# A decay table from Exps alone or from Exps and products, and the queues of the first chunk's loads

## The chip, the cores and the metric

The kernel runs on one core of a Trainium2 chip. The metric is the device time of one execution in microseconds (us). Most executions of one kernel here agree within 0.3%; all runs named below were in the fast state, except one single look whose state is unknown.

## The reference

A retention layer (4 batches, 8 heads, 768 positions, head size 64) feeds a gated feed-forward layer (3072 tokens, 512 wide, 1536 inside):

```python
for t in range(S):
    state = gamma[None, :, None, None] * state + np.einsum('bhd,bhe->bhde', k[:, :, t], v[:, :, t])
    y[:, :, t] = scale * np.einsum('bhd,bhde->bhe', q[:, :, t], state)
...
gate = 1.0 / (1.0 + np.exp(-(x @ w_gate)))
val = x @ w_val
return (gate * val @ w_out).astype(np.float32)
```

The decay `gamma` differs by head. The kernel works in chunks of 128 positions, six per batch. It scales v by a table that rises with the position (`tabv`, the decay's reciprocal) and the result by one that falls (`taby`, the decay itself, one column per position), so that the products between need no decay.

## The kernel before

Each chunk goes through: loads, transposes of k and q on TensorE, a copy of them to SBUF, the on-chip memory, on ScalarE (`qkT`), scores on TensorE, masks on VectorE, the state's product on TensorE and its cast on ScalarE (`zbd`), the intra products, and `y_out` on VectorE, which multiplies by `taby`. The first chunks are run one by one while the weights are loaded, with filler matmuls (`keep_on`) to keep TensorE's clock up. From chunk 3 on, attention is interleaved with the feed-forward layer.

```python
    nc.sync.dma_start(out=kf, in_=src(k, 0))
    nc.scalar.dma_start(out=qf, in_=src(q, 0))
    load_v(0, nc.sync)
    ...
    def make_taby(cols):
        for p in range(NP):
            nc.scalar.activation(taby[:, p, cols], toky[:, cols], AX.Exp, scale=lgp[:, p:p + 1], bias=lsc)
    ...
    def scale_v(g, eng):          # two SBUF inputs
        eng.tensor_tensor(vs[g], vf[g], tabv[...].to_broadcast([C, H, D]), op=ALU.mult)
    ...
    make_taby(slice(0, 256))
    nc.vector.tensor_copy(kn[0], kf)
    nc.scalar.copy(qn[0], qf)
    keep_on(36)
    transposes(0)
    keep_on(8)
    scale_v(0, nc.vector)
    scores(0); state(0); state_out(0); masks(0)
    keep_on(8)
    make_taby(slice(256, 384))
    transposes(1)
    ...                            # chunk 1: make_taby(slice(384, 512)) in front of transposes(2)
    make_taby(slice(512, 768))     # chunk 2
    nc.scalar.preload_act_table(AX.Sigmoid)
```

All other loads go through GpSimd's queue, in the order of use, with weights between the chunks.

Of the kernel before, what the change touches and what calls it, by code (L numbers as in the profile page):

```python
# [9 lines left out]
F32 = mybir.dt.float32  # L10
BF16 = mybir.dt.bfloat16
I32 = mybir.dt.int32
AX = mybir.ActivationFunctionType
ALU = mybir.AluOpType
# [3 lines left out]
def kernel(  # L18
# [10 lines left out]
    nc = tc.nc  # L29
    B, H, S, D = q.shape  # L30
# [4 lines left out]
    NP = H // 2  # L35
    KT = D_MODEL // 128
    NFF = D_FF // 128
    scale = 1.0 / math.sqrt(D)
    lg = [math.log(1.0 - 2.0 ** (-5.0 - h)) for h in range(H)]

    ctx.enter_context(tc.manual_schedule())
    const = ctx.enter_context(tc.tile_pool(name="const", bufs=1))
# [12 lines left out]
    def src(x, g):  # L55
        b, c = divmod(g, NCH)
        return x[b, :, c * C:(c + 1) * C, :].rearrange("h s d -> s h d")

    def load_v(g, eng):
        vf[g] = ld.tile([C, H, D], F32, tag="vf", name="vf", bufs=8)  # L60
        eng.dma_start(out=vf[g], in_=src(v, g))  # L61

    def load_kq(g):
        kn[g] = ld.tile([C, H, D], BF16, tag="kn", name="kn")
        qn[g] = ld.tile([C, H, D], BF16, tag="qn", name="qn")
        nc.gpsimd.dma_start(out=kn[g], in_=src(k, g))  # L66
        nc.gpsimd.dma_start(out=qn[g], in_=src(q, g))  # L67

    def load_chunk(g):
        load_kq(g)  # L70
        load_v(g, nc.gpsimd)
# [5 lines left out]
    def load_gate_val(s):  # L77
        cols = slice(s * 256, (s + 1) * 256)
        for dst, w in ((wg, moe_w_gate), (wv, moe_w_val)):
            nc.gpsimd.dma_start(out=dst[:, :, cols],  # L80
                                in_=w.rearrange("(kk p) n -> p kk n", p=128)[:, :, cols])
# [6 lines left out]
    kf = const.tile([C, H, D], F32, name="kf")  # L88
    qf = const.tile([C, H, D], F32, name="qf")
    nc.sync.dma_start(out=kf, in_=src(k, 0))  # L90
    nc.scalar.dma_start(out=qf, in_=src(q, 0))
    load_v(0, nc.sync)
    tokv = const.tile([128, NCH], I32, name="tokv")
    nc.gpsimd.iota(tokv, pattern=[[C, NCH]], base=0, channel_multiplier=1)
    ident = const.tile([128, 128], BF16, name="ident")
    make_identity(nc, ident)
    toky = const.tile([128, S], I32, name="toky")
    nc.gpsimd.iota(toky, pattern=[[1, S]], base=0, channel_multiplier=0)
    load_chunk(1)
    causal = const.tile([128, 128], F32, name="causal")  # L100
    nc.gpsimd.memset(causal, 1.0)
# [7 lines left out]
    lgp = const.tile([128, NP], F32, name="lgp")  # L109
    lsc = const.tile([128, 1], F32, name="lsc")  # L110
    nc.vector.memset(lsc, math.log(scale))
    for p in range(NP):
        nc.vector.memset(lgp[0:D, p:p + 1], lg[2 * p])
        nc.vector.memset(lgp[D:128, p:p + 1], lg[2 * p + 1])
    zbd = [const.tile([128, NP, C], BF16, name=f"zbd{i}") for i in range(2)]
    for t in zbd:
        nc.vector.memset(t, 0.0)
    taby = const.tile([128, NP, S], F32, name="taby")

    def make_taby(cols):  # L120
        for p in range(NP):
            nc.scalar.activation(taby[:, p, cols], toky[:, cols], AX.Exp, scale=lgp[:, p:p + 1], bias=lsc)  # L122

    causal4 = causal.unsqueeze(1).to_broadcast([128, NP, 128])

# [7 lines left out]
    def transposes(g):  # L133
        tp = pa.tile([128, 2 * NP, C], BF16, tag="tp", name="tp")
        for i, x in enumerate((kn[g], qn[g])):
            for p in range(NP):
                nc.tensor.transpose(tp[:, i * NP + p, :], pair(x, p), ident)  # L137
        qkT[g] = at.tile([128, 2 * NP, C], BF16, tag="qkT", name="qkT", bufs=3)
        nc.scalar.activation(qkT[g], tp, AX.Copy)  # L139
# [15 lines left out]
    def masks(g):  # L155
        stA[g] = at.tile([128, NP, C], BF16, tag="stA", name="stA")
        stB[g] = at.tile([128, NP, C], BF16, tag="stB", name="stB")
        nc.vector.tensor_tensor(stA[g], sc[g][0], causal4, op=ALU.mult)  # L158
        nc.vector.tensor_tensor(stB[g], sc[g][1], causal4, op=ALU.mult)  # L159
# [8 lines left out]
    def state(g):  # L168
        b, c = divmod(g, NCH)
        if c == 0:  # L170
            zps[b] = pa.tile([128, NP, D], F32, tag="z", name="z", padded_shape=[128, NP, C])
        if c < NCH - 1:
            for p in range(NP):
                for i in range(2):
                    nc.tensor.matmul(zps[b][i * D:(i + 1) * D, p, :], kn[g][:, 2 * p + i, :], vs[g][:, 2 * p + i, :],  # L175
                                     start=(c == 0 and p == 0), stop=True, skip_group_check=True)

    def state_out(g):
        b, c = divmod(g, NCH)
        if c < NCH - 1:  # L180
            for i in range(2):
                half = slice(i * D, (i + 1) * D)
                nc.scalar.copy(zbd[g % 2][half, :, half], zps[b][half])  # L183

    def intra(g):
        first = g % NCH == 0
        for p in range(NP):
            for i, st in enumerate((stA[g], stB[g])):
                nc.tensor.matmul(y[g][i * D:(i + 1) * D, p, :], vs[g][:, 2 * p + i, :], st[:, p, :],  # L189
                                 start=(first and p == 0), stop=True, skip_group_check=True)  # L190
# [60 lines left out]
    def keep_on(n):  # L251
        u = pf.tile([128, 512], F32, tag="ff", name="ff")
        for _ in range(n):
            nc.tensor.matmul(u[:, :128], ident, ident, start=True, stop=True)  # L254


    load_gate_val(0)
    load_chunk(3)
    for s in range(1, NFF // 2):
        load_gate_val(s)  # L260
    load_chunk(4)
    for s in range(4):
        load_out(s)
# [2 lines left out]

    kn[0] = ld.tile([C, H, D], BF16, tag="kn", name="kn")
    qn[0] = ld.tile([C, H, D], BF16, tag="qn", name="qn")
    make_taby(slice(0, 256))
    nc.vector.tensor_copy(kn[0], kf)  # L270
    nc.scalar.copy(qn[0], qf)
    keep_on(36)
# [3 lines left out]
    scores(0)  # L276
    state(0)
    state_out(0)
    masks(0)
    keep_on(8)  # L280
    make_taby(slice(256, 384))
    transposes(1)
    scale_v(1, nc.vector)
    inter(0)
# [6 lines left out]
    masks(1)  # L291
    inter(1)
    keep_on(10)
    make_taby(slice(384, 512))
    transposes(2)
    intra(1)
    scale_v(2, nc.vector)
# [5 lines left out]
    masks(2)  # L303
    inter(2)
    keep_on(12)
    make_taby(slice(512, 768))
    nc.scalar.preload_act_table(AX.Sigmoid)  # L307
    intra(2)
    y_out(2)
    scale_v(3, nc.vector)  # L310
# [62 lines left out]
```

## Time and profile before

| what | value | where |
|---|---|---|
| time | 248.32 us (248.23 to 248.34) | three runs, the median first; a fourth, taken with the result, makes it 248.30 |
| span of the profiled run, mean granted clock | 246.4 us, 0.997 | page, list of cores |
| TensorE busy | 95% | page |
| Exps of the table between chunks | 5.37 us | timeline of ScalarE |
| k, q and v of chunk 0 land at | 4.6, 5.3, 6.6 us | issue plus time to landing |
| scores of chunks 0, 1, 2 start at | 7.54, 11.76, 15.98 us | timeline of TensorE |
| first up matmul | 18.98 us | timeline of TensorE |

In a line of a timeline the first number is the start and the second the duration, in us; then come engine, source line, operation, output and inputs. A bracket at the end gives how long the engine had been idle and what ended that. Source lines shift by 8 between the two kernels: the copy qkT is L139 before and L147 after, the scaling of v L143 and L151.

### The profile page before, as it was taken

The page shows a single profiled execution, that of the slowest core. Times are in us where ns is not written, and L with a number is a line of the kernel's source. Part 1 is how long each engine was busy: PE and PEld are TensorE (multiplying, and loading weights), DVE is VectorE, ACT ScalarE, POOL GpSimd, SP SyncE. Part 2 cuts the span into 40 slices and gives each one's busy share as a digit, 9 for nine tenths or more (in the row PEclk, how much of TensorE's full clock was granted, in tenths as well). Part 3 has the DMA queues.
Part 4 walks back from the last instruction along what each step waited for, and adds up shares of the span by engine and source line. Part 5 has one row for each costly group of instructions (what it writes and reads, how often), then busy time and mean ns, then how long its engine had stood idle before and what let it go on. Part 6 is the DMA issues. An engine that isn't in the chain of part 4 may idle for free.

```text
span 246.4 us, 4449 instructions
## 1 busy us (share of the span) xinstructions
PE 234.1 (95%) x1816; PEld 123.3 (50%) x1816; DVE 101.5 (41%) x168; ACT 106.0 (43%) x191; POOL 91.5 (37%) x111
## 2 busy tenths in 40 slices
PE   7689998997999999999999999999999999999993
PEld 7565644554455554445554445544445554444441
DVE  2565444563446631246631256541256532234300
ACT  7788333425444431454443444342444542233221
POOL 8986574987999912961111001111000000000000
PEclk9999999999999999999999999999999999999998
DMA  9999999999999932994012100002100002200022
GB/s 146 181 198 196 192 213 203 176 208 232 229 174 127 188 80 84 145 180 61 3 41 78 54 3 3 0 17 92 64 0 3 0 0 88 85 0 3 0 85 85
DMA packets 64212, 24.13 MB, mean 98 GB/s; under 512 B 51969, under 2 KB 59649, under 8 KB 64193
## 3 DMA queue, kind: packets, MB, share of 16 engines
q0 software_dynamic: 57616, 16.78, 62.2%
q1 hardware_dynamic: 5536, 6.82, 8.2%
q10 hardware_dynamic: 1040, 0.26, 0.5%
q8 instruction: 14, 0.23, 0.4%
q14 instruction: 6, 0.04, 0.1%
HBM read 28.31 MB, written 6.29 MB: 140 GB/s over the span
## 4 chain that ended last, share of the span: by engine, by line
PE 91%; ACT 7%; issue 1%; DVE 0%; POOL 0%; POOLq 0%; ACTq 0%
PE ff L234 50%; PE ff L244 26%; PE tp L137 4%; PE sA L153 3%; ACT qkT L139 2%; PE y L189 2%; ACT taby L122 2%; PE z L175 2%; PE y L165 2%; PE ff L254 2%; ACT zbd L183 1%; ACT L307 1%; ACT ob L247 0%; ACT gs L238 0%; DVE xT L197 0%
## 5 line engine op out<-in xcount | busy, mean ns | idle before, releaser
L239 DVE TENSOR_TENSOR hT<-gs,ff 128x512 bf16<-128x512 f32 (+2 forms) x76 | 50.1, 660 | 85.6 <-PE ff L234 81.9
L234 PE MATMUL ff<-xT,wg 128*128 128x512 bf16 (+2 forms) x304 | 74.7, 368 | 1.2 <-DVE xT L197 1.1
L234 PE MATMUL ff<-xT,wv 128*128 128x512 bf16 (+2 forms) x304 | 74.6, 368 | 0.0
L238 ACT ACTIVATE gs<-ff 128x512 f32<-128x512 f32 (+2 forms) x76 | 43.6, 573 | 55.4 <-PE ff L234 55.4
L244 PE MATMUL ff<-wo,hT 128*128 128x512 bf16 x288 | 65.0, 379 | 0.0
L234 PEld LDWEIGHTS <-wv 128*128 128x128 bf16 x304 | 29.3, 98 | 33.2
L244 PEld LDWEIGHTS <-hT 128*128 128x128 bf16 x288 | 27.3, 98 | 32.1
L234 PEld LDWEIGHTS <-wg 128*128 128x128 bf16 x304 | 27.4, 98 | 28.4 <-issue 1.4
L143 POOL TENSOR_TENSOR vs<-vf,tabv 128x512 bf16<-128x512 f32 x16 | 16.6, 1058 | 65.0 <-PE y L189 60.1
L247 ACT COPY ob<-ff 128x512 f32<-128x512 f32 x24 | 14.1, 586 | 54.9 <-PE ff L244 50.5
L139 ACT ACTIVATE qkT<-tp 128x1024 bf16<-128x1024 bf16 x24 | 24.6, 1024 | 13.4 <-PE tp L137 13.3
L197 DVE TENSOR_TENSOR xT<-y,taby 128x512 bf16<-128x512 f32 x24 | 16.4, 684 | 20.6 <-PE y L189 20.6
L158 DVE TENSOR_TENSOR stA<-sA,causal 128x512 bf16<-128x512 f32 x24 | 16.5, 687 | 19.9 <-PE sB L153 19.9
L61 POOL DMA_DIRECT2D vf<-in_v_dram x23 | 21.0, 913 | 5.0 <-issue 2.0
L66 POOL DMA_DIRECT2D kn<-in_k_dram x23 | 21.0, 913 | 3.3 <-DMA wo<-in_moe_w_out_dram 1.7
L67 POOL DMA_DIRECT2D qn<-in_q_dram x23 | 20.6, 897 | 2.6 <-DMA wo<-in_moe_w_out_dram 1.7
L183 ACT CAST zbd<-z 64x256 bf16<-64x256 f32 x40 | 14.7, 367 | 12.1 <-PE z L175 11.8
L159 DVE TENSOR_TENSOR stB<-sB,causal 128x512 bf16<-128x512 f32 x24 | 16.3, 680 | 0.0
L153 PE MATMUL sA<-qkT 64*128 64x128 bf16 x96 | 9.5, 219 | 5.5 <-ACT qkT L139 5.4
L153 PEld LDWEIGHTS <-qkT 64*128 64x128 bf16 x192 | 5.4, 94 | 10.6 <-ACT qkT L139 6.8
L254 PE MATMUL ff<-ident 128*128 128x128 bf16 x104 | 9.0, 252 | 1.6 <-POOL ident masks.py:199 1.6
L189 PE MATMUL y<-stA,vs 128*64 128x128 bf16 x96 | 9.9, 222 | 0.0
(36 smaller groups left out, 123.1 us busy)
## 6 DMA issues: line engine op xcount, KB each, us to landing
out_dram<-ob SPq DMA_DIRECT2D x24, 256.0 KB, 2.0
vf<-in_v_dram POOLq DMA_DIRECT2D x23, 256.0 KB, 7.2
kn<-in_k_dram POOLq DMA_DIRECT2D x23, 128.0 KB, 7.2
qn<-in_q_dram POOLq DMA_DIRECT2D x23, 128.0 KB, 7.1
wg<-in_moe_w_gate_dram POOLq DMA_DIRECT2D x6, 256.0 KB, 8.7
wv<-in_moe_w_val_dram POOLq DMA_DIRECT2D x6, 256.0 KB, 9.2
wo<-in_moe_w_out_dram POOLq DMA_DIRECT2D x4, 384.0 KB, 10.7
qf<-in_q_dram ACTq DMA_DIRECT2D x1, 256.0 KB, 4.5
```

The source lines that it names most:

```text
L61: eng.dma_start(out=vf[g], in_=src(v, g))
L66: nc.gpsimd.dma_start(out=kn[g], in_=src(k, g))
L67: nc.gpsimd.dma_start(out=qn[g], in_=src(q, g))
L139: nc.scalar.activation(qkT[g], tp, AX.Copy)
L143: eng.tensor_tensor(vs[g], vf[g], tabv[:, g % NCH, :].unsqueeze(2).to_broadcast([C, H, D]), op=ALU.mult)
L153: nc.tensor.matmul(sc[g][i][:, p, :], t[half, p, :], t[half, NP + p, :], start=True, stop=True)
L158: nc.vector.tensor_tensor(stA[g], sc[g][0], causal4, op=ALU.mult)
L183: nc.scalar.copy(zbd[g % 2][half, :, half], zps[b][half])
L234: nc.tensor.matmul(u[:, lo:hi], w[:, kk, n1 * 128:(n1 + 1) * 128], xT[t][:, kk, lo:hi], start=(kk == 0), stop=(kk == KT - 1))
L238: nc.scalar.activation(gs[:, lo:hi], ps[0][:, lo:hi], AX.Sigmoid)
L239: nc.vector.tensor_tensor(hT[t][:, n1, lo:hi], gs[:, lo:hi], ps[1][:, lo:hi], op=ALU.mult)
L244: nc.tensor.matmul(o, hT[t][:, n1, sm * 128:(sm + 1) * 128], wo[:, n1, :], start=(n1 == 0), stop=(n1 == NFF - 1))
```

## The change

It means to take the table's Exps out of ScalarE's path between chunks: exp(a + 256 d) is exp(a) times a constant of the head, so the columns from 256 on become two products on GpSimd. With that, the second table load can go earlier. The other part moves q of chunk 0 to SyncE's queue, behind k, and v to ScalarE's, behind the first table load, so that k and q come first.

```diff
     nc.sync.dma_start(out=kf, in_=src(k, 0))
-    nc.scalar.dma_start(out=qf, in_=src(q, 0))
-    load_v(0, nc.sync)
+    nc.sync.dma_start(out=qf, in_=src(q, 0))
+    nc.scalar.preload_act_table(AX.Exp)
+    load_v(0, nc.scalar)
...
-    toky = const.tile([128, S], I32, name="toky")
+    toky = const.tile([128, 256], I32, name="toky")
...
+    for p in range(NP):
+        nc.scalar.activation(taby[:, p, 0:256], toky, AX.Exp, scale=lgp[:, p:p + 1], bias=lsc)
+
+    def extend_taby(i):
+        nc.gpsimd.tensor_tensor(taby[:, :, i * 256:(i + 1) * 256], taby[:, :, 0:256],
+                                gup[i].unsqueeze(2).to_broadcast([128, NP, 256]), op=ALU.mult)
...
     load_gate_val(0)
+    extend_taby(1)
     load_chunk(3)
     for s in range(1, NFF // 2):
         load_gate_val(s)
+    extend_taby(2)
     load_chunk(4)
...
     state_out(0)
+    nc.scalar.preload_act_table(AX.Sigmoid)
...
-    make_taby(slice(256, 384))
-    make_taby(slice(384, 512))
-    make_taby(slice(512, 768))
-    nc.scalar.preload_act_table(AX.Sigmoid)
```

More of the change, by code (lines that the diff above doesn't have):

```diff
@@ L96 @@
     make_identity(nc, ident)
-    toky = const.tile([128, S], I32, name="toky")
-    nc.gpsimd.iota(toky, pattern=[[1, S]], base=0, channel_multiplier=0)
+    toky = const.tile([128, 256], I32, name="toky")
+    nc.gpsimd.iota(toky, pattern=[[1, 256]], base=0, channel_multiplier=0)
     load_chunk(1)
@@ L114 @@
         nc.vector.memset(lgp[D:128, p:p + 1], lg[2 * p + 1])
+    gup = {i: const.tile([128, NP], F32, name=f"gup{i}") for i in (1, 2)}
+    for i, t in gup.items():
+        for h in range(H):
+            nc.vector.memset(t[h % 2 * D:(h % 2 + 1) * D, h // 2:h // 2 + 1], math.exp(256 * i * lg[h]))
     zbd = [const.tile([128, NP, C], BF16, name=f"zbd{i}") for i in range(2)]
@@ L118 @@
     taby = const.tile([128, NP, S], F32, name="taby")
-    def make_taby(cols):
-        for p in range(NP):
-            nc.scalar.activation(taby[:, p, cols], toky[:, cols], AX.Exp, scale=lgp[:, p:p + 1], bias=lsc)
+    for p in range(NP):
[3 more added lines that the diff above has]
+                                gup[i].unsqueeze(2).to_broadcast([128, NP, 256]), op=ALU.mult)
     causal4 = causal.unsqueeze(1).to_broadcast([128, NP, 128])
@@ L268 @@
     qn[0] = ld.tile([C, H, D], BF16, tag="qn", name="qn")
-    make_taby(slice(0, 256))
     nc.vector.tensor_copy(kn[0], kf)
```

## The prediction

> **What bounds the kernel now.** I read the page first, then the chain of waits in order of time for the first 25 us, then the timelines of ScalarE, TensorE, VectorE and GpSimd there, and at last the DMA issues one by one. The page says that TensorE is the bound of the whole, and that ScalarE is on the path only for a few per cent:
>
> ```profile
> ## 4 chain that ended last, share of the span: by engine, by line
> PE 91%; ACT 7%; issue 1%; DVE 0%; POOL 0%; POOLq 0%; ACTq 0%
> PE ff L234 50%; PE ff L244 26%; PE tp L137 4%; PE sA L153 3%; ACT qkT L139 2%; PE y L189 2%; ACT taby L122 2%; PE z L175 2%; PE y L165 2%; PE ff L254 2%; ACT zbd L183 1%; ACT L307 1%; ACT ob L247 0%; ACT gs L238 0%; DVE xT L197 0%
> ```
>
> The table's Exps (L122) and the second table load (L307) are together 3% of 246.4 us, some 6 to 7 us. The timeline of ScalarE shows where they stand: between the cast of the state (zbd) and the copy of the next chunk's transposes (qkT), which the scores wait for.
>
> ```profile
> 8.22 0.76 ACT L183 CAST zbd<-z 64x256 bf16<-64x256 f32 x2 [0.74 <-PE z L175]
> 9.01 1.65 ACT L122 ACTIVATE taby<-toky,lsc,lgp 128x128 f32<-128x128 int32 x4
> 10.68 1.02 ACT L139 ACTIVATE qkT<-tp 128x1024 bf16<-128x1024 bf16 x1
> ...
> 13.22 1.65 ACT L122 ACTIVATE taby<-toky,lsc,lgp 128x128 f32<-128x128 int32 x4
> 14.90 1.02 ACT L139 ACTIVATE qkT<-tp 128x1024 bf16<-128x1024 bf16 x1
> ...
> 17.47 2.07 ACT L122 ACTIVATE taby<-toky,lsc,lgp 128x256 f32<-128x256 int32 x4
> 19.57 1.28 ACT L307 ACT_TABLE_LOAD   x1
> 20.86 0.49 ACT L238 ACTIVATE gs<-ff 128x384 f32<-128x384 f32 x1
> ```
>
> What the reader is to see: after zbd there is never a gap, the table follows, then qkT. Columns are start, duration, engine, line. A second resource is full there: page line "DMA" has nines from the start up to about 90 us. Where data come just in time, I find by setting each landing (issue start plus time to landing) beside its first use. The tightest later one is chunk 5's q: its issue on GpSimd, and its use on TensorE:
>
> ```profile
> 32.88 0.87 POOL L67 DMA_DIRECT2D qn<-in_q_dram  x1
> ```
>
> ```profile
> qn<-in_q_dram POOLq DMA_DIRECT2D x1, 128.0 KB, 10.8
> ```
>
> ```profile
> 44.49 0.39 PE L137 MATMUL tp<-ident,kn 128*128 128x128 bf16 x4
> 44.72 0.39 PE L137 MATMUL tp<-ident,qn 128*128 128x128 bf16 x4
> ```
>
> It lands at 32.88 + 10.8 = 43.7 and is used at 44.72, only 1.0 us later. For chunk 5's k it is 31.95 + 10.7 = 42.65 against 44.49, 1.8 us; for chunk 6's q 36.35 + 10.3 = 46.65 against 48.88, 2.2 us; for the weight slices in between 5 us and more.
>
> **What the Trainium skill says.** "ScalarE: Activation LUTs", section "What ACT_TABLE_LOAD costs", gives 1283 ns for a load and about 1380 ns of drain with it. The trace has 1.28 us, and the next ACTIVATE 0.01 us later; no drain shows here, so I count 1.28. "GPSIMD Engine Reference", section 3.1, gives 4497 ns for a two-input fp32 tensor_tensor of 2048 columns, so an estimate of 2.2 us for 1024; the trace's own row (vs on POOL, 512 columns, 1058 ns) gives 2.1, which agrees. "SBUF — State Buffer", section "Who interferes with whom", says that a VectorE instruction with two SBUF inputs and a GpSimd one that reads SBUF exclude each other for a whole instruction. The trace before has no such pair overlapping, so no row shows it. "DMA: Bandwidth & Descriptors", section "Queues, rings and completion order", says that an engine takes turns between rings, which is what putting k and q on one ring and v on another plays with.
>
> **The change part by part.**
> *Removed from ScalarE:* 1.65 + 1.65 + 2.07 = 5.37 us of Exps between chunks, and the table load at 19.57. The first four Exps (2.06 us) stay, and one table load of 1.28 is put in the place of the first removed group.
> *First chunk:* kn is cast at 4.68 when k lands, q's cast starts at 5.35 when the first Exps end, and q lands at 0.80 + 4.5 = 5.3. With the load issued first, ScalarE may be up to 0.45 us earlier, but TensorE's 36 filler matmuls end at 5.6 in any case. v of chunk 0 may land later, and it can hold the first state up. I count 0 ± 0.4.
> *Chunk 1:* after zbd ends at 8.98 comes the load of 1.28 where Exps of 1.65 stood, so qkT(1) starts at 10.3 in place of 10.68: 0.4 gained.
> *Chunk 2:* nothing stands between now. Shifted by 0.4, the transposes end at 13.34, qkT(2) runs 13.35 to 14.4. TensorE still has the intra products and 12 fillers to do, which end at about 14.45. Scores at 14.45 in place of 15.98: 1.5 gained. So the removed 1.65 is hardly worth more than 1.1, because TensorE's own fillers become the bound.
> *End of chunk 2:* the Exps of 2.07 and the load of 1.28 stood beside VectorE's masks and y_out, not alone: the up matmuls waited for xT until 18.98. Only from 19.79 to 20.86 did a sigmoid wait for the load. Working the order of instructions forward with the durations of before (up(0,0) at 17.45, qkT(3) 19.4 to 20.4, scores(3) at 20.5 behind up(0,1), in place of 22.32) gives 1.8; VectorE's v scaling waits for chunk 3's v (11.59 + 7.0 = 18.6) and takes a little back: 1.7 by 24.6.
> *Added to GpSimd:* two products of 2.1 us. The first stands in front of chunk 3's loads, which go out at about 11.5 in place of 9.85. Then wv's first slice (9.12 + 6.6 = 15.7) is still under way, so the DMA engines don't run dry, and later issues wait for landings anyway (0.2 to 1.0 us each from 15.97 on), so the delay is absorbed. The second lies among those waits too. The shorter iota saves some 0.5 us at the first issue, of which 0 to 0.4 reaches the landings. VectorE gets 16 memsets at 0.1 us a step, before k lands: nothing.
> *At 42 to 44 us:* with TensorE 1.7 early, chunk 5's q would be wanted at 43.0 and lands at 43.7 less 0 to 0.4. It stalls 0.3 to 0.7 and leaves 1.0 to 1.4. From there on TensorE is full to the end as before, and nothing more is won.
> *Sum:* 0.4 + 1.1 + 0.2 − 0.5 = 1.2 us; rounded for the first chunk's doubt, 248.3 − 1.1 = 247.2.
>
> **The rivals.**
> *(a) The whole 5.4 + 1.3 us comes off.* The chain of waits books them so. Against it: the fillers and VectorE lie just under it, and the landings cap it at 1.0 to 1.4 whatever the first 25 us give. It would make 242 to 243.
> *(b) The port lock.* The first product runs from about 9.4 to 11.5, and vs(1) on VectorE, with two SBUF inputs, is ready at about 9.6 when chunk 1's v lands. If the product gets in first, vs(1) goes to 11.5, and y_out(0) and masks(1) behind it: masks end at about 14.05 in place of 13.1, scores(2) at 15.25, a gain there of 0.7, about 1.0 by 25 us. Then the stall at chunk 5 is nil, so the end is nearly the same: 247.3 to 247.6. It depends on tenths which is first; I give it six in ten.
> *(c) v of chunk 0 comes late* behind the table load, or q shares its turn with v and lands after 6: the first chunk loses up to 0.8, but much of it lies under (b). 247.5 to 248.3.
> *(d) GpSimd becomes the bound,* its late issues reaching the landings: chunk 5's q later by up to 2 us would make 248 to 250. The waits for landings speak against it.
>
> **Range and chances.** (b) and the sum above give 247.0 to 247.6; (c) stretches it up, more luck with the landings down. Range 246.4 to 248.0. A gain of 2% needs 5 us, which only (a) gives; a loss of 2% needs something that no view shows.
>
> **What would show it.** Right: no L122 behind a zbd in ScalarE's timeline; a table load of 1.28 behind the first zbd; scores(2) at 14.4 to 15.3; up(0,0) near 17.5 to 18.3; chunk 5's q landing within 0.5 us of 43.7 and TensorE waiting there, or just not; from 50 us on all stages early by about 1.1. With (b), vs(1) on VectorE starts or lasts beyond 11 us. Wrong: landings that move by over 1 us, in either direction, for then the cap moves; or a stage after 50 us that isn't shifted like the rest.

## The result

The changed kernel took 248.58 us (median of four runs, 248.31 to 249.23) against 248.30 for the kernel before. Its ratio to the kernel before is 1.0015, with a 95% interval of 0.9996 to 1.0035. Here and below such a ratio is the mean time of one kernel's fast runs over that of the other's of the same rounds, so it is not quite the ratio of the medians. The predicted 247.2 and its range of 246.4 to 248.0 missed: nothing was gained.

The table's Exps have gone from ScalarE's timeline, as intended, yet the chunks start no earlier. This is the timeline of ScalarE in the changed kernel:

```profile
6.64 0.62 ACT L280 CAST qn<-qf 128x512 bf16<-128x512 f32 x1 [1.69 <-DMA qf<-in_q_dram]
7.75 1.02 ACT L147 ACTIVATE qkT<-tp 128x1024 bf16<-128x1024 bf16 x1 [0.49 <-PE tp L145]
9.83 0.76 ACT L191 CAST zbd<-z 64x256 bf16<-64x256 f32 x2 [1.06 <-PE z L183]
10.60 1.28 ACT L288 ACT_TABLE_LOAD   x1
11.90 1.02 ACT L147 ACTIVATE qkT<-tp 128x1024 bf16<-128x1024 bf16 x1
...
14.99 1.02 ACT L147 ACTIVATE qkT<-tp 128x1024 bf16<-128x1024 bf16 x1 [0.57 <-PE tp L145]
```

The cast of q now waits 1.69 us for its load and starts at 6.64, against 5.35 before. In the kernel before these two instructions stood here:

```profile
5.35 0.61 ACT L271 CAST qn<-qf 128x512 bf16<-128x512 f32 x1
6.46 1.02 ACT L139 ACTIVATE qkT<-tp 128x1024 bf16<-128x1024 bf16 x1 [0.49 <-PE tp L137]
```

The copies qkT start 1.29 us later for chunk 0, 1.22 for chunk 1, and 0.09 for chunk 2 (7.75, 11.90 and 14.99 against 6.46, 10.68 and 14.90). What the missing Exps won, 1.1 us of it at chunk 2, paid for what chunk 0 had lost. At the first fully shared stage nothing is left: the transposes of chunk 5 start at 44.60, before at 44.49.

The loads of chunk 0, from the DMA issues of the kernel before and then of the changed one (queue, operation, size, us from issue to landing):

```profile
qf<-in_q_dram ACTq DMA_DIRECT2D x1, 256.0 KB, 4.5
kf<-in_k_dram SPq DMA_DIRECT2D x1, 256.0 KB, 3.8
vf<-in_v_dram SPq DMA_DIRECT2D x1, 256.0 KB, 5.3
```

```profile
kf<-in_k_dram SPq DMA_DIRECT2D x1, 256.0 KB, 3.8
vf<-in_v_dram ACTq DMA_DIRECT2D x1, 256.0 KB, 4.5
qf<-in_q_dram SPq DMA_DIRECT2D x1, 256.0 KB, 5.3
```

The three times are the same; q and v have changed places. In both kernels the load that stands first on its queue lands at 4.6 or 5.3 us, and the one that stands second lands at 6.6. The table load did not hold v back: the timeline of ScalarE shows why.

```profile
0.80 1.28 ACT L92 ACT_TABLE_LOAD   x1 [0.80 <-PEq L363]
0.83 0.48 ACTq L61 DMA_DIRECT2D vf<-in_v_dram  x1
```

The issue on ScalarE's queue (ACTq) goes out at 0.83, while the load of 1.28 us runs. So v went off beside k, and q had to wait behind k. This agrees with the turns between rings (the queues of the issuing engines) that the Trainium skill, "DMA: Bandwidth & Descriptors", section "Queues, rings and completion order", describes. The trace before already had the number: there v, second on SyncE's queue with q's load beside, landed at 6.6.

A second effect follows on TensorE. In the table of stretches by engine, the columns are the window, its length, busy time and count on TensorE, its weight loads, VectorE, ScalarE and GpSimd, then the granted clock, DMA share and GB/s:

```profile
8.00:9.00 1.00, 0.33 (x7) 0.18 (x6) 0.00 (x0) 0.77 (x1) 1.00 (x2) 0.85 1.89 149
9.00:10.00 1.00, 1.00 (x19) 0.74 (x16) 0.46 (x1) 0.17 (x1) 1.00 (x2) 0.50 2.37 177
10.00:11.00 1.00, 1.00 (x13) 1.00 (x11) 1.00 (x3) 0.96 (x3) 1.00 (x1) 0.50 1.20 196
```

After TensorE had waited 1.56 us for q's cast and 0.67 us for qkT, its clock was at half speed for some 3 us (8.7 to 12.1, by windows of 0.2 us). The kernel before has 1.00 in all these windows.

### The profile page after: what moved, and what is told of

Same layout as the page of the kernel before. It is cut to its first block, busy times and chain, and to the rows that moved or that the text cites. A ratio compares the mean times of both kernels' runs of the same rounds, so it can differ in the third digit from the quotient of the medians.

```text
span 246.5 us, 4430 instructions
## 1 busy us (share of the span) xinstructions
PE 233.5 (95%) x1789; PEld 124.1 (50%) x1816; DVE 102.7 (42%) x184; ACT 100.8 (41%) x179; POOL 94.8 (38%) x113
## 3 DMA queue, kind: packets, MB, share of 16 engines
q1 hardware_dynamic: 5536, 6.82, 8.2%
HBM read 28.31 MB, written 6.29 MB: 140 GB/s over the span
## 4 chain that ended last, share of the span: by engine, by line
PE 90%; ACT 3%; DMA 2%; DVE 2%; issue 1%; SPq 0%; ACTq 0%; DVEq 0%
PE ff L242 50%; PE ff L252 25%; PE tp L145 4%; PE sA L161 3%; PE y L197 3%; DMA qf<-in_q_dram 2%; PE y L173 2%; PE z L183 2%; ACT qkT L147 2%; ACT ob L255 1%; PE ff L262 1%; DVE xT L205 1%; DVE vs L151 0%; DVE stA L166 0%; ACT qn L280 0%
## 5 line engine op out<-in xcount | busy, mean ns | idle before, releaser
L242 PE MATMUL ff<-xT,wg 128*128 128x512 bf16 (+2 forms) x291 | 73.4, 368 | 1.8 <-DVE xT L205 1.1
L252 PE MATMUL ff<-wo,hT 128*128 128x512 bf16 x279 | 64.2, 379 | 0.6 <-issue 0.2
L145 PE MATMUL tp<-ident,qn 128*128 128x128 bf16 x96 | 9.5, 223 | 1.6 <-ACT qn L280 1.6
```

The lines of the kernel that those rows point to most:

```text
L145: nc.tensor.transpose(tp[:, i * NP + p, :], pair(x, p), ident)
L242: nc.tensor.matmul(u[:, lo:hi], w[:, kk, n1 * 128:(n1 + 1) * 128], xT[t][:, kk, lo:hi], start=(kk == 0), stop=(kk == KT - 1))
L252: nc.tensor.matmul(o, hT[t][:, n1, sm * 128:(sm + 1) * 128], wo[:, n1, :], start=(n1 == 0), stop=(n1 == NFF - 1))
```

## The experiments

Two theories stood at the start. Theory Q: the queues took the gain back. Rival P: the products on GpSimd did, by keeping VectorE waiting. Nine kernels were run, in three sets, each set on one chip with its own runs of the kernel before (medians 248.28, 248.18 and 248.26 us). All gave the right result.

| kernel | time, us | ratio to before (95%) | scores of chunk 2 | chunk 5's q transposed |
|---|---|---|---|---|
| before | 248.2 to 248.3 | 1 | 15.98 | 44.72 |
| changed | 248.58 | 1.0015 (0.9996 to 1.0035) | 16.07 | 44.83 |
| e1 old queues | 247.71 | 0.9976 (0.9963 to 0.9988) | 15.24 | 43.98 |
| e2 queues only | 250.12 | 1.0068 (1.0056 to 1.0081) | 17.67 | 46.41 |
| e3 fillers in the gap | 248.31 | 1.0002 (0.9989 to 1.0014) | 15.94 | 44.69 |
| e4 all on SyncE | 247.76 | 0.9981 (0.9967 to 0.9994) | 15.60 | 44.35 |
| e5 products on VectorE | 247.61 | 0.9975 (0.9962 to 0.9989) | 14.56 | 43.89 |
| e6 e5, chunk 5 early | 246.63 | 0.9937 (0.9925 to 0.9950) | 14.50 | 42.98 |
| e7 probe | 251.71, one look | none | none | none |
| e8 e1, chunk 5 early | 247.77 | 0.9978 (0.9964 to 0.9991) | 15.25 | 44.01 |
| e9 e6, fewer fillers | 246.65 | 0.9934 (0.9921 to 0.9946) | 14.16 | 42.64 |

### e1: the old queues

```diff
-    nc.sync.dma_start(out=qf, in_=src(q, 0))
+    nc.scalar.dma_start(out=qf, in_=src(q, 0))
     nc.scalar.preload_act_table(AX.Exp)
-    load_v(0, nc.scalar)
+    load_v(0, nc.sync)
```

> The changed kernel, but with the first chunk's loads on the queues of before (k, then v on SyncE's, q on ScalarE's, ahead of the table load). Theory Q (the queues took the gain back: q landed at 6.6 us in place of 5.3, and TensorE's clock fell while it waited): q lands near 5.3, no slice of the first 20 us has a granted clock under 0.95, scores of chunk 2 start at 14.4 to 15.3 in place of 16.07, and the time is 0.7 to 1.4 us under the kernel before, 246.9 to 247.6. Rival P (the products on GpSimd and the port lock took the gain back): about the time of the kernel before, 248.0 to 248.6, with scores of chunk 2 at 15.7 or later.

q landed at 5.3, the clock stayed at 1.00, and the time fell to 247.71, which is 0.57 us under the kernel before in medians and 0.87 under the changed kernel. So the queues had taken back more than the rest of the change gives. The time is a little above what I had expected for Q, and a part of P shows in VectorE's timeline:

```profile
6.73 1.86 DVE L151 TENSOR_TENSOR vs<-vf,tabv 128x512 bf16<-128x512 f32 x1 [1.61 <-DMA vf<-in_v_dram]
8.52 0.68 DVE L166 TENSOR_TENSOR stA<-sA,causal 128x512 bf16<-128x512 f32 x1
9.12 0.68 DVE L167 TENSOR_TENSOR stB<-sB,causal 128x512 bf16<-128x512 f32 x1
9.34 1.95 POOL L129 TENSOR_TENSOR taby<-taby,gup 128x1024 f32<-128x1024 f32 x1
9.72 2.13 DVE L151 TENSOR_TENSOR vs<-vf,tabv 128x512 bf16<-128x512 f32 x1
```

The scaling of v takes 0.69 us before; here it takes 1.86 for chunk 0 and 2.13 for chunk 1. The second lies beside the product on GpSimd, as rival (b) of the prediction had it. The first doesn't: it ends before the profile's start of the product. The masks, with one input in PSUM (the memory that TensorE's results stand in), are not stretched, not even the one beside the product.

What the two stretches cost is read on TensorE and ScalarE, here and then in e6, which has neither (below):

```profile
8.65 0.32 PE L183 MATMUL z<-vs,kn 128*64 128x64 bf16 x8 [0.69 <-DVE vs L151]
9.00 0.76 ACT L191 CAST zbd<-z 64x256 bf16<-64x256 f32 x2 [1.50 <-PE z L183]
```

```profile
8.25 0.76 ACT L191 CAST zbd<-z 64x256 bf16<-64x256 f32 x2 [0.74 <-PE z L183]
```

The state's product waits for the first stretched scaling, and zbd comes 0.75 us later than in e6. The scores of chunk 2 come 0.74 later (15.24 against 14.50), so the second stretch adds nothing there.

### e2: the queues alone

The kernel before with only the three lines of the queues changed.

> The kernel before with nothing changed but the queues and the first table load ahead of them. Theory Q: q lands at 6.6, its transposes wait for it, and the time is 1.0 to 2.5 us over the kernel before, 249.3 to 250.8, with a clock near 0.5 for some 3 us if the drop follows the gap. Rival P: within 0.3 us of the kernel before.

It took 250.12 us, 1.84 over the kernel before. q landed at 1.29 + 5.6 = 6.9 and its cast started at 6.90. Here ScalarE's Exps still stand in each chunk, and the delay goes through to the end: qkT starts 1.55, 1.70 and 1.69 us late for chunks 0, 1 and 2. The clock fell here too (0.50 from 10 to 12 us). So this part of the change alone is a loss, and Q holds.

### e3: fillers in the gap

```diff
+            if g == 0 and i == 0:
+                keep_on(26)
...
     transposes(0)
-    keep_on(8)
+    keep_on(16)
```

> The changed kernel with 26 more filler matmuls between the transposes of k and those of q of chunk 0, and 8 more after them, so that TensorE is not idle while q is awaited. q still lands at 6.6. Theory Q, the part of it about the clock: the granted clock stays over 0.95, the work from 8.8 to 12.1 us runs at full pace, and the time is 0.3 to 1.0 us under that of the changed kernel, 247.6 to 248.3. If the clock's drop costs nothing because other waits cover it: 248.5 as the changed kernel.

The clock stayed at 1.00 in these stretches, and the state's cast of chunk 0 came 1.76 us after qkT's start in place of 2.08, so the fall of the clock costs 0.32 there. It isn't covered later: from qkT's start of chunk 0 to the scores of chunk 2 it is 8.01 us here and 8.32 in the changed kernel. These scores come only 0.13 earlier (15.94 against 16.07) because q landed later in this profile (its cast starts at 6.82, there at 6.64). The time, 248.31, is 0.27 under the changed kernel's, but the two intervals overlap. And two of the four runs of the changed kernel have a mean clock of 0.998 and 0.999 and yet took 249.23 and 248.65. So the clock's fall, some 0.3 us in the profiled run, is the smaller part, and the late q, which is still there, is the larger one. My lower bound for the gain, 0.3 us, wasn't reached clearly.

### e4: k, q and v on one queue

```diff
     nc.scalar.preload_act_table(AX.Exp)
-    load_v(0, nc.scalar)
+    load_v(0, nc.sync)
```

> The changed kernel with k, q and v of chunk 0 all on SyncE's queue, in this order. If the engines share their time between rings as the trace suggests, k and q land before v: k at 4.0 to 4.6, q at 5.0 to 5.5, v at 6.4 to 6.9. Theory Q: the same as with the old queues, 246.9 to 247.6. If the landing of q depends on its place behind k and not on v's ring: q at 6 or later and 248.5.

k landed at 4.1 and q at 5.3, as in the first reading. v landed at 1.92 + 5.9 = 7.8, a microsecond later than I had expected, and the scaling of v waited for it. So second place on a queue is not itself what delayed q: it depends on what the other queue carries. The time is 247.76, nearly that of e1 and a little above the expected range. The clock fell to 0.50 from 9.2 to 12.4 us in the profiled run here too, after two waits of 0.67 and 0.91 us, and the run was no slower than 0.2 us over its median: again little.

### e5: the products on VectorE

From e1, the calls moved and the engine changed:

```diff
-        nc.gpsimd.tensor_tensor(taby[:, :, i * 256:(i + 1) * 256], taby[:, :, 0:256],
+        nc.vector.tensor_tensor(taby[:, :, i * 256:(i + 1) * 256], taby[:, :, 0:256],
...
     nc.vector.tensor_copy(kn[0], kf)
+    extend_taby(1)
...
     for n1 in range(4):
         up(0, n1, 384, 512)
+    extend_taby(2)
```

> As e1 (old queues, the rest of the change), but the two products run on VectorE, the first right behind the cast of chunk 0's k, where VectorE waits for v, the second behind the last 128-column up group; GpSimd only issues loads. Theory L (in e1 the products on GpSimd kept VectorE's scaling of v waiting: 1.86 and 2.13 us in place of 0.69): the products take about 1.1 us each, all scalings take 0.69, scores of chunk 2 start at 14.4 to 14.7 in place of 15.24 and the time is 0.4 to 0.9 us under e1, 246.8 to 247.3, unless chunk 5's q, landing near 43.8, gives part back. Rival R (the stretched scalings are covered by other waits): the time of e1, 247.5 to 247.9.

The first product took 1.22 us in VectorE's wait for v, and the scalings of chunks 0 and 1 took 0.69 again, so both stretches belong to the products on GpSimd. TensorE was 0.9 us ahead of e1 when the first 512-column up group began (26.94 against 27.88). The time, 247.61, is still e1's. TensorE's timeline shows where the lead stays:

```profile
42.91 0.40 PE L145 MATMUL tp<-ident,kn 128*128 128x128 bf16 x4
43.89 0.40 PE L145 MATMUL tp<-ident,qn 128*128 128x128 bf16 x4 [0.58 <-DMA qn<-in_q_dram]
44.12 2.75 PE L252 MATMUL ff<-wo,hT 128*128 128x512 bf16 x12
```

It waits for chunk 5's q, which lands at 32.99 + 10.9 = 43.9. That is the cap that the prediction had put at 43.7. Against the kernel before, 0.83 us of the lead are left there (43.89 against 44.72).

### e6: chunk 5 ahead of the output weights

```diff
     load_chunk(4)
+    load_chunk(5)
     for s in range(4):
         load_out(s)
-    for g in range(5, 8):
+    for g in range(6, 8):
```

> As e5, with the loads of chunk 5 moved ahead of those of the output weights. Theory C (the landing of chunk 5's k and q caps the gain, as the prediction had it): chunk 5's q lands near 37 to 39 and TensorE doesn't wait at 42 to 44, and the time is 0.2 to 0.8 us under e5, 246.2 to 246.9, unless the output weights, now some 3 us later, are late for the first down group. Rival: no cap, the same as e5 within 0.15 us.

Chunk 5's q lands at 28.04 + 8.6 = 36.6 and is transposed at 42.98 without a wait. The time is 246.63, 1.0 us under e5, somewhat more than expected. It is the first version that is clearly ahead of both kernels, by 0.6% of the kernel before: its interval lies well below 1.

### e7: when is VectorE locked out?

From e1, with 40 products of four columns, each with two SBUF inputs, behind the cast of chunk 0's k. Its time means nothing.

```diff
     nc.vector.tensor_copy(kn[0], kf)
+    probe = const.tile([128, 160], F32, name="probe")
+    for i in range(40):
+        nc.vector.tensor_tensor(probe[:, 4 * i:4 * i + 4], gup[1], gup[2], op=ALU.mult)
```

> As e1, with 40 tiny VectorE products of two SBUF inputs (4 columns each) behind the cast of chunk 0's k, to see when VectorE's second read is locked out; the time itself means nothing. Theory L with cores that run ahead (the first product on GpSimd begins on most of its cores long before the start that the profile gives, 9.34[...]): the small ones run at 0.1 us or less until about 6, then one of them lasts some 1.9 us, to about 7.9, and they are fast again. Rival (a load issue of GpSimd, or something else, stretched the scaling of chunk 0's v in e1): no long one near 6 to 8, or several short stretches at each load issue.

The median of the 40 is 0.15 us in the record, of which neighbours overlap. Two are long, from VectorE's timeline, and only one product stands in GpSimd's, below them:

```profile
6.29 1.93 DVE L282 TENSOR_TENSOR probe<-gup,gup 128x4 f32<-128x4 f32 x1
```

```profile
9.51 1.96 DVE L282 TENSOR_TENSOR probe<-gup,gup 128x4 f32<-128x4 f32 x1
```

```profile
6.24 0.89 POOL L67 DMA_DIRECT2D qn<-in_q_dram  x1
7.11 0.92 POOL L61 DMA_DIRECT2D vf<-in_v_dram  x1
7.99 0.79 POOL L80 DMA_DIRECT2D wg<-in_moe_w_gate_dram  x1
8.73 0.79 POOL L80 DMA_DIRECT2D wv<-in_moe_w_val_dram  x1
9.48 1.96 POOL L129 TENSOR_TENSOR taby<-taby,gup 128x1024 f32<-128x1024 f32 x1
```

The second lockout has the product's own times, and it is exclusive: a product of four columns waits for all of 1024. The first is as long and starts 3.2 us before the profile's start of the product, while GpSimd's row shows only load issues. e5 has the same load issues and no product there, and no stretch. So the product on GpSimd is what keeps VectorE waiting both times. That some of GpSimd's cores run ahead, past the load issues, would fit this: the Trainium skill, "GPSIMD Engine Reference", section 2.1, says that a core starts the next instruction when its own share is done, and "Perfetto Trace Analysis", section "GPSIMD Engine Instruction", that the start shown is core 0's first read. Two lockouts of one product agree with both, but no run shows single cores, so this reading stays open.

### e8: e6 with the products on GpSimd

e1 with e6's order of loads; the edit is e6's.

> As e6 (chunk 5's loads early), but with the products back on GpSimd, as in e1. e1 and e5 took the same time, 247.71 and 247.61, though VectorE's scalings are stretched only in e1. Theory L with C (in e5 the late q of chunk 5 hid what the products on VectorE had won): here nothing hides it, so this one is as e1, 247.5 to 247.8, and 0.8 to 1.1 us over e6's 246.63; the scaling of chunk 0's v lasts about 1.9 and that of chunk 1's about 2.1 us again. Rival R (the lock costs no time): as e6, 246.5 to 246.9.

It took 247.77 us, 1.14 over e6, with the scalings of chunks 0 and 1 at 1.94 and 2.13 us. Once nothing later caps the lead, the products on GpSimd are seen to cost 1.1 us. Of this, 0.75 stand at the scores of chunk 2 (15.25 against 14.50), by the first stretched scaling as in e1, and 1.03 at chunk 5's q (44.01 against 42.98); which part the rest is (the second product, or the loads issued behind the products), no run separates. The equal times of e1 and e5 had been two different limits of the same size.

### e9: fewer fillers

```diff
-    nc.scalar.dma_start(out=qf, in_=src(q, 0))
     nc.scalar.preload_act_table(AX.Exp)
+    nc.scalar.dma_start(out=qf, in_=src(q, 0))
...
-    keep_on(10)
     transposes(2)
...
-    keep_on(12)
+    keep_on(8)
     scores(2)
```

> As e6, with the first table load ahead of q's issue on ScalarE, the 10 filler matmuls in front of chunk 2's transposes gone, and 8 in place of 12 behind them. Theory: in e6 ScalarE idles 0.57 us before chunk 2's copy (qkT) because the transposes stand behind fillers; without them the copy starts at about 12.9 in place of 13.4 and the time is 0.2 to 0.6 us under e6, 246.0 to 246.4. If TensorE's clock falls for want of fillers, or masks set the pace: the same as e6 or slower.

The scores of chunk 2 came 0.34 us earlier than in e6 and the clock stayed up, but the time is e6's, 246.65. The lead is still there at 42.64 and is given back in the first down group, where TensorE now waits for the last output weights, and at chunk 6's transposes, which both kernels start at 46.91:

```profile
45.14 0.81 PE L252 MATMUL ff<-wo,hT 128*128 128x512 bf16 x3 [0.17 <-DMA wo<-in_moe_w_out_dram]
46.91 0.40 PE L145 MATMUL tp<-ident,kn 128*128 128x128 bf16 x4
```

So my expectation failed on the next landing, and it was that of the weights. The step behind this down group, the product of `zbd`, starts at 45.78 here and at 45.79 in e6, so all of the 0.34 us is gone before chunk 6's transposes; the last weights land at 34.13 + 11.0 = 45.1.

## Why the prediction was wrong

**The bound.** Right: ScalarE's Exps stood on the path in the first 20 us, and the landings bound the time right behind.

**First chunk: the step that failed.** The prediction counted "0 ± 0.4". It measured 1.29 us late at qkT(0). q's place behind k on one queue moved its landing from 5.3 to 6.6, because v, on the other queue, went out beside k at 0.83. The prediction held it possible that v comes late behind the table load, and named the other case only in rival (c), with up to 0.8 us, "much of it" under (b). The mechanism of (c) was right. Its size was too small, and it was the other way round with (b): in the changed kernel chunk 0's v is scaled at 5.43, ahead of where e7 has the first lockout (6.29), and VectorE then waits 3.42 us for the late scores; chunk 1's scaling takes 1.12 and ends at 11.86, ahead of its use at 13.30. So the late q hid the lock. e1, without it, is 0.87 us faster than the changed kernel, and e2, with it alone, is 1.84 slower than the kernel before. TensorE's idle time there also brought the clock down, which no step had; e3 puts that at 0.31 us up to chunk 2's scores.

**Chunk 1.** Right in its own term: from zbd's end to qkT's start, the load of 1.28 took the place of 1.65, and the delay fell from 1.61 us at zbd to 1.22 at qkT.

**Chunk 2.** Right: 1.1 us gained there (1.22 late at chunk 1, 0.09 at chunk 2), and e6 with both disturbances gone has its scores at 14.50, against the 14.45 predicted.

**End of chunk 2.** In e6 scores(3) stand at 20.58 (predicted: 20.5) and the lead there is 1.74 us (predicted: 1.8).

**Added to GpSimd.** The products took 1.96 and 1.91 us (predicted: 2.1), and the late issues behind them didn't reach the landings: chunk 5's q was issued at 33.03 against 32.88. Rival (d) was rightly set aside. Rival (b), the lock, came true in e1 in another way than told: the second lockout is the one that I described, and it cost nothing at chunk 2's scores; the first hit chunk 0's scaling and, by zbd, made the whole delay. That the gain left there is the 0.7 that (b) gave (e1: 15.24 in place of 15.98; predicted: 15.25) is luck.

**At 42 to 44 us.** Right: e5 shows the stall, and e6 what lies behind it. In e5 the lead falls from 1.58 us at chunk 5's k to 0.83 at its q, a little more than the 0.3 to 0.7 predicted.

**The sum.** At chunk 2's scores the books close: 1.48 us that the change could gain (e6: 14.50 against 15.98), less 1.29 for q and 0.31 for the clock, is a loss of 0.12, and 0.09 was measured. But the first chunk on time would not have given 1.2 us either. e5, with it on time and no lock, keeps the 0.83 us, where the prediction left 1.0 to 1.4, and its time is only 0.57 under the kernel before.

What lies between 0.83 and 0.57 is outside the profile. The time is longer than the profiled span by 1.66 to 1.76 us in every run of the kernel before in the three sets, and of e2. In the changed kernel and in each of e1, e3 to e6, e8 and e9 it is longer by 1.9 to 2.0 on average (e7's one look: 1.71). So the change to the table, and not that to the queues, mostly goes with 0.2 to 0.3 us that no view shows; why is left open. The spans of the changed kernel and of the kernel before (in e1's set) have the same median, 246.6 us.

## What to carry to other kernels

When a load is made second on a queue, ask what the other queue carries meanwhile: q behind k landed at 6.6 us with v beside it, and at 5.3 with v behind it (e4). An instruction in front of the other queue's load need not hold that load back: the table load didn't (0.83). Read the landings, not the source order. An elementwise product moved to GpSimd was not free for VectorE's instructions with two SBUF inputs, and the first lockout began 3.2 us before the product's row in the profile (e7). When two fixes seem to be worth nothing, undo the next limit (here a landing at 44 us) before judging them.

## What the Trainium skill lacked or had wrong

- "GPSIMD Engine Reference" (section 2.1) and "SBUF — State Buffer" ("Who interferes with whom"): both give the parts, but no page says that a GpSimd product behind load issues can lock VectorE out twice, the first time 3.2 us before its start in the profile (6.29 to 8.22 and 9.51 to 11.47, product 9.48 to 11.44). The exclusive lock itself is confirmed.
- "ScalarE: Activation LUTs" ("What ACT_TABLE_LOAD costs"): the drain of about 1380 ns didn't show as added time; the load took 1.28 us, and qkT followed 0.02 us later (10.60, then 11.90).
- "TensorE: Matmul & The Clock Gate" ("Why this matters for your kernels") warns of idle gaps over some 3 us; here the clock fell after gaps of 1.56 and 0.67 us within 3.1 us, and in e4 after 0.67 and 0.91 us, while gaps of 1.33 and 1.12 us in the kernel before left it at 1.00. The runs give no rule for it.
